# Induced attention with a maxout layer, one core: an output copy in four and two small additions go from ScalarE to VectorE

## The chip, the core and the metric

The kernel runs on one core of one Trainium2 chip. The metric is device time in microseconds (us) of one execution, as the median of repeated runs. The core's engines are TensorE (PE in the views, its weight loads PEld), VectorE (DVE), ScalarE (ACT), GpSimd (POOL) and SyncE (SP), which here issues transfers. They run side by side, each through its own list of instructions in order, and wait for each other by semaphores.

## The reference, cut to what matters

```python
def _attn_ref(x, inducing):                 # x: 4 x 12544 x 128, inducing: 32 x 128
    I = np.broadcast_to(inducing[None], (B, m, C))
    def mab(q, kv):
        s = scale * (q @ kv.transpose(0, 2, 1))
        s = s - s.max(-1, keepdims=True)
        a = np.exp(s)
        a /= a.sum(-1, keepdims=True) + 1e-09
        return a @ kv
    h = mab(I, x)
    return mab(x, h)

def _moe_ref(x, w1, w2, w3, w_out):         # x: 50176 x 128, w1..w3: 128 x 768, w_out: 768 x 128
    h = np.maximum(np.maximum(x @ w1, x @ w2), x @ w3)
    return h @ w_out
```

For each of four batches, 32 inducing vectors attend over 12544 tokens (the first attention); every token then attends over the 32 results (the second attention); and each token's result goes through a layer that keeps the largest of three products and multiplies it by `w_out`.

## The kernel before

**Slots.** The second attention's weights (32 numbers per token, as a high and a low part, in the tiles `pT`) are multiplied with matrices `us` made beforehand for the batch. The work is cut into chunks of 512 tokens and, within a chunk, into six slots (`j` from 0 to 5) of 128 hidden units. There are 600 slots. In each of them TensorE makes `pu` and `pv` (lines 790 and 800); ScalarE turns `pu` into `ru` with a Relu (809); VectorE takes the larger of `pv` and `ru` as `h` (830); ScalarE rounds `h` to `hi` (819); and the remainder `h - hi` goes into `lows`, which GpSimd makes for most slots (827) and VectorE for a few (833, by the tables `LOWVEC` and `LOWLAST`). Six slots later TensorE adds `hi` and `lows` times `w_out` up in `acc` (862 to 864). After a chunk's last slot, `finish` copies `acc` to `o` (875) and SyncE sends it out.

**Windows.** A batch is one short group of two 128-token tiles and six full groups of four chunks, of which the chunks count as `q` = 0 to 3. 24 slots make a window, in which one full group passes. I number the steps of a window 0 to 23. At fixed steps of it the attention work is put between the slots:

- the softmax of the second attention for the next group (`scores_steps`): transpose at step 3, maximum at 5, subtraction at 7, exponential on ScalarE at 8, row sums `rs` at 9, the addition of 1e-9 to `rs` at 10, reciprocal and multiplication at 11, transpose back at 13, rounding `ph` on ScalarE at 14, remainder `pl` at 15. In the last window of a batch two groups of the next batch pass through it, the short one a step earlier.
- the first attention of the next batch (not in the last batch): maximum, weights (449), transposes, sums, and `attend_add`, which adds a group's sums to the running ones: `hs` on VectorE (540), and the running sum of the weights in `lst` (543).
- TensorE's own part of the attention comes as bursts, the main one at step 2 (lines 696, 366, 502).

**Order.** All five lists are in the order in which the Python code calls the instructions. Within a step, `advance()` issues for ScalarE the next slot's `ru` and then the last slot's `hi`, and for VectorE `h` and then a `lows`, if there is one. After that comes `finish` of the chunk that has just ended (steps 0, 6, 12 and 18; `q` = 0 ends at step 12), and last the attention's entries for the step.

**Buffers that tie the engines.** `pu` and `pv` have two banks each: a slot's `pu` waits for the `ru` of two slots before, its `pv` for the `h` of two slots before. There are five buffers for `h`, ten for `hi`, eight for `lows`. `pu`, `pv`, `acc` and the attention's banks (`aux`) lie in PSUM; `ru`, `h`, `hi`, `lows`, `rs`, `lst` and `o` in SBUF.

Of the kernel before, what the change touches and what calls it, by code (L numbers as in the profile page):

```python
# [8 lines left out]
F32 = mybir.dt.float32  # L9
# [3 lines left out]
AF = mybir.ActivationFunctionType  # L13
ALU = mybir.AluOpType
# [11 lines left out]
def kernel(ctx, tc, x, xt, ind_t, w1, w2, w3, w_out, out):  # L26
    nc = tc.nc
# [3 lines left out]
    P = 128  # L31
# [19 lines left out]
    scale = 1.0 / float(C) ** 0.5  # L51
# [66 lines left out]
        (16, 10, "t", 3, 6),  # L118
    )
    LOWVEC = (23, 0, 15, 18)  # L120
    LOWLAST = (23, 0, 9, 15, 18)
    UW = 2 * DF + C
    UQ = UW // NQ

# [3 lines left out]
    while t0 < NT:  # L128
        nt = NT % GT if t0 == 0 and NT % GT else GT
# [6 lines left out]
    const = ctx.enter_context(tc.tile_pool(name="const", bufs=1))  # L136
# [55 lines left out]
    def first_load(what):  # L192
# [12 lines left out]
        out=sel[:, :M], in_=ident.rearrange("p (q m) -> p m q", m=M), axis=AX.X, op=ALU.add  # L205
    )
    nc.vector.tensor_copy(
        out=sel[:, M:].rearrange("p (q m) -> p q m", m=M),
        in_=sel[:, :M].unsqueeze(1).to_broadcast([P, NQ - 1, M]),
# [1 line left out]
    quad = const.tile([P, NQ], F32, name="quad")  # L211
    nc.vector.tensor_reduce(out=quad, in_=ident.rearrange("p (q m) -> p q m", m=M), axis=AX.X, op=ALU.add)

    eps = const.tile([P, 1], F32, name="eps")
    nc.gpsimd.memset(eps, 1e-9)

    bands = const.tile([P, NQ + 1, M], F32, name="bands")
    nc.gpsimd.memset(bands, 0.0)
# [152 lines left out]
    def opens(b, gi):  # L371

        return b > 0 and gi == 1
# [155 lines left out]
    def attend_add(b, gi):  # L529
        st = state[b]  # L530
        h = st["h"].pop(gi)
        if opens(b, gi):
            nc.scalar.copy(out=st["hs"], in_=h)
            if b == 1:
                st["l1"] = st["lst"][:, 1:2]
                return
            st["l1"] = st["lst"][:, :1]
            nc.scalar.activation(out=st["l1"], in_=st["l1"], func=AF.Identity, bias=st["lst"][:, 1:2])
            return
        nc.vector.scalar_tensor_tensor(  # L540
            out=st["hs"], in0=st["hs"], scalar=st["al"], in1=h, op0=ALU.mult, op1=ALU.add
        )
        nc.scalar.activation(
            out=st["l1"], in_=st["l1"], func=AF.Identity, scale=st["al"], bias=st["lst"][:, gi : gi + 1]
        )

    def add_quadrants(st):
# [133 lines left out]
    def sorted_(ap):  # L681

        return ap.rearrange("p (b a) -> p a b", a=2)

    def halves(ap):

        return ap.rearrange("p (a b) -> p a b", a=2)
# [13 lines left out]
    def scores_steps(b, gi):  # L701

        nt = groups[gi]["nt"]
        w = nt * M
        st = state[b]
        sp = st["s"].pop(gi)
        flat = sp[:, :w]
        ev = flat.rearrange("p (t m) -> p t m", m=M)
        nc.vector.transpose(out=flat, in_=flat)
        yield  # L710
        mx = wk.tile([P, GT], F32, name="mx", tag="mx")
        nc.vector.tensor_reduce(out=mx[:, :nt], in_=ev, axis=AX.X, op=ALU.max)
        yield
        nc.vector.tensor_sub(out=ev, in0=ev, in1=mx[:, :nt].unsqueeze(2).to_broadcast([P, nt, M]))
        yield
        nc.scalar.activation(out=flat, in_=flat, func=AF.Exp, scale=scale)
        yield
        rs = wk.tile([P, GT], F32, name="rs", tag="rs")
        nc.vector.tensor_reduce(out=rs[:, :nt], in_=ev, axis=AX.X, op=ALU.add)
        yield  # L720
        if b == 0 and gi < 2:
            nc.vector.tensor_scalar_add(out=rs[:, :nt], in0=rs[:, :nt], scalar1=1e-9)
        else:
            nc.scalar.activation(out=rs[:, :nt], in_=rs[:, :nt], func=AF.Identity, bias=eps)
        yield
        nc.vector.reciprocal(out=rs[:, :nt], in_=rs[:, :nt])
        nc.vector.tensor_mul(out=ev, in0=ev, in1=rs[:, :nt].unsqueeze(2).to_broadcast([P, nt, M]))
        yield
        if nt < GT:

            pn = wk.tile([P, nt, 2, 2, M], F32R, name="pn", tag="pn", bufs=1)
            e4 = ev.unsqueeze(2).to_broadcast([P, nt, 2, M])
            nc.scalar.copy(out=pn[:, :, :, 0, :], in_=e4)
            yield
            nc.vector.tensor_sub(out=pn[:, :, :, 1, :], in0=e4, in1=pn.bitcast(F32)[:, :, :, 0, :])
            st[("p", gi)] = pn
            yield
            return
        nc.vector.transpose(out=flat, in_=flat)
        yield  # L740
        ph = wk.tile([P, 512], F32R, name="ph", tag="ph")
        nc.scalar.copy(out=ph, in_=flat)
        yield
        pl = wk.tile([P, 512], F32R, name="pl", tag="pl")
        nc.vector.tensor_sub(out=pl, in0=flat, in1=ph.bitcast(F32))
        st[("p", gi)] = (ph.bitcast(F32), pl.bitcast(F32))
        yield
# [87 lines left out]
    class Chunk:  # L835
# [7 lines left out]
        def low(self, k):  # L843
# [3 lines left out]
            if self.b == 0 and self.gi == 1:  # L847
                return NJ * self.q + k in LOWVEC[:1]
            return NJ * self.q + k in (LOWVEC if self.b + 1 < B else LOWLAST)

# [14 lines left out]

    def finish(c):
        at = groups[c.gi]["at"] + (c.q or 0) * c.w
        turns = [(nc.vector.tensor_copy if c.n < 3 else nc.scalar.copy, nc.sync)]
        if len(c.acc) > 1:

            turns = [(nc.vector.tensor_copy, nc.sync), (nc.scalar.copy, nc.scalar)]
        for (acc, cs), (copy, queue) in zip(c.acc, turns):
            o = op.tile([P, 512], F32, name="o", tag="o", bufs=3)
            w = cs.stop - cs.start
            copy(out=halves(o[:, :w]), in_=sorted_(acc[:, :w]))  # L875
            queue.dma_start(out=out[c.b, :, at + cs.start : at + cs.stop], in_=o[:, :w])
# [27 lines left out]
    def softmax2(b, gi, *when):  # L904

        gen = []

        def step():
            if not gen:
                gen.append(scores_steps(b, gi))  # L910
            next(gen[0], None)

        for s in when:
            at(s, step)
# [60 lines left out]
    for n, turns in enumerate(TURNS, start=1):  # L975
        for gi, win, slot, wait, past in turns:
            s = begins(win) + slot
            if gi:
                burst(s, (attend_products, n, gi, bank_a[1]))
                if gi == 1:  # L980
                    burst(s, (attend_products, n, 0, None, 2 * P))
                    at(s + 1, keep_short, n)
                softmax1(n, gi, s, wait, calm=2 * narrow(s))
            for k, g in enumerate(past):
                burst(s, (attend_sums, n, g, None, k * P))
                at(s + 1 + (k if len(past) > 1 else narrow(s)), attend_add, n, g)
        s = begins(win) + (8 if slot < 8 else 20)
        at(s, add_quadrants, ("state", n))
        at(s, total_sums, ("state", n))
        at(s + 1, invert_total, ("state", n))  # L990
        at(s + 1, combine_states, ("state", n), 1)
# [160 lines left out]
```

## Time and profile before

| | |
|---|---|
| median of 3 runs | 790.11 us (790.03 to 791.17) |
| the profiled execution | 790.35 us |
| its span, first to last instruction | 788.5 us |
| TensorE busy | 774.7 us, 98% of the span |
| ScalarE busy | 727.1 us, 92% |
| VectorE busy | 639.4 us, 81% |
| GpSimd busy | 639.6 us, 81% |
| granted TensorE clock, mean | 0.999 |

The profile is of one execution. Busy time is the time in which an engine has at least one instruction under way. ScalarE's and VectorE's instructions overlap a little with the next one, so what an instruction takes up of its engine is the distance from its start to the next one's start where nothing is waited for. TensorE's matmuls are pipelined, so its busy share says little; there, too, the distance from start to start is what counts. Idle time in the views stands with what ended it.

### The profile page before, as it was taken

Reading aid. Unit: us, or ns where it says so; the run is one execution under the profiler, and the core shown is the slowest. Engines: PE = TensorE matmul, PEld = TensorE weight load, DVE = VectorE, ACT = ScalarE, POOL = GpSimd, SP = SyncE. Lnnn points to the kernel's source line nnn. Section 1 sums busy time; section 2 is a strip of 40 time slices with the busy share of each in tenths; the row PEclk is TensorE's granted clock in tenths of the full one; section 3 lists DMA queues with packets and bytes.
Section 4 is the critical chain, followed back from the end, with each engine's and each line's share of the span. In section 5 each row is a group of like instructions: output and inputs, shape, how many; then the busy total and the mean of one; then the engine's idle time right before and its main releaser. Section 6 shows DMA issues by size and latency. Waiting matters only on the chain.

```text
span 788.5 us, 14348 instructions
## 1 busy us (share of the span) xinstructions
PE 774.7 (98%) x4567; PEld 626.4 (79%) x4567; DVE 639.4 (81%) x1071; ACT 727.1 (92%) x1529; POOL 639.6 (81%) x523
## 2 busy tenths in 40 slices
PE   8999999999999999999999999999999999999998
PEld 6768878878787787787878877878888788787887
DVE  5898978878877787887887878878888788888876
ACT  5789899999998999998998999999999999999996
POOL 1379879878788897887987978879879989888887
PEclk9999999999999999999999999999999999999999
DMA  9744325274542643543644336334223222222221
GB/s 355 293 148 126 100 91 178 62 249 161 189 139 65 200 131 101 188 123 108 217 137 132 114 103 195 120 114 134 71 79 96 74 81 81 68 87 73 69 81 53
DMA packets 52266, 102.24 MB, mean 130 GB/s; under 512 B 18144, under 2 KB 21344, under 8 KB 46944
## 3 DMA queue, kind: packets, MB, share of 16 engines
q1 hardware_dynamic: 52048, 101.21, 40.5%
q8 instruction: 36, 0.59, 0.3%
q14 instruction: 38, 0.31, 0.1%
q10 hardware_dynamic: 144, 0.13, 0.0%
HBM read 48.12 MB, written 25.69 MB: 94 GB/s over the span
## 4 chain that ended last, share of the span: by engine, by line
PE 56%; ACT 33%; POOL 3%; DMA 3%; DVE 2%; issue 1%; SPq 0%; POOLq 0%; ACTq 0%; DVEq 0%
ACT ru L809 14%; ACT hi L819 13%; PE pu L790 10%; PE acc L862 9%; PE pv L800 9%; PE acc L863 9%; PE acc L864 9%; PE aux L696 3%; POOL lows L827 3%; ACT o L875 2%; PE acc L502 2%; DMA raw<-in_w_dram 2%; PE aux L366 2%; PE acc L861 2%; ACT aux L449 1%
## 5 line engine op out<-in xcount | busy, mean ns | idle before, releaser
L827 POOL TENSOR_TENSOR lows<-h,hi 128x512 fp32r<-128x512 f32 (+1 forms) x504 | 624.4, 1275 | 112.4 <-ACT hi L819 109.3
L830 DVE TENSOR_TENSOR h<-pv,ru 128x512 f32<-128x512 f32 (+1 forms) x600 | 400.9, 673 | 123.8 <-PE pv L800 63.0
L809 ACT ACTIVATE ru<-pu 128x512 f32<-128x512 f32 (+1 forms) x600 | 407.0, 679 | 37.8 <-PE pu L790 37.5
L819 ACT CAST hi<-h 128x512 fp32r<-128x512 f32 (+1 forms) x596 | 416.3, 699 | 0.3 <-DVE h L830 0.2
L790 PE MATMUL pu<-pT,us 128*128 128x512 f32 (+1 forms) x600 | 229.2, 382 | 4.5 <-ACT ru L809 3.7
L800 PE MATMUL pv<-pT,us 128*128 128x512 f32 (+1 forms) x600 | 226.6, 378 | 1.6 <-DVE h L830 1.5
L862 PE MATMUL acc<-hi,wo_hi 128*128 128x512 f32 (+1 forms) x594 | 225.5, 380 | 0.0
L863 PE MATMUL acc<-hi,wo_lo 128*128 128x512 f32 (+1 forms) x594 | 222.6, 375 | 0.0
L864 PE MATMUL acc<-lows,wo_hi 128*128 128x512 f32 (+1 forms) x594 | 222.6, 375 | 0.0
L790 PEld LDWEIGHTS pu<-pT,us 128*128 128x128 f32 x600 | 113.2, 189 | 37.8 <-ACT ru L809 18.8
L862 PEld LDWEIGHTS acc<-hi,wo_hi 128*128 128x128 f32 x594 | 112.2, 189 | 21.9 <-issue 7.5
L800 PEld LDWEIGHTS pv<-pT,us 128*128 128x128 f32 x600 | 113.4, 189 | 19.6 <-DVE h L830 6.6
L864 PEld LDWEIGHTS acc<-lows,wo_hi 128*128 128x128 f32 x594 | 112.3, 189 | 15.3
L863 PEld LDWEIGHTS acc<-hi,wo_lo 128*128 128x128 f32 x594 | 112.3, 189 | 14.7
L833 DVE TENSOR_TENSOR lows<-h,hi 128x512 fp32r<-128x512 f32 x96 | 87.7, 913 | 0.8 <-ACT hi L819 0.8
L875 ACT COPY o<-acc 128x512 f32<-128x512 f32 (+1 forms) x96 | 65.3, 680 | 0.0
L861 PE MATMUL acc<-pT,us 128*128 128x512 f32 (+1 forms) x99 | 37.3, 376 | 0.0
L502 PEld LDWEIGHTS acc<-xg,aT 128*32 128x32 f32 x640 | 18.0, 110 | 9.6 <-issue 5.4
L696 PE MATMUL aux<-xT,hT 128*32 128x512 f32 x192 | 25.1, 603 | 0.0
L366 PE MATMUL aux<-xT,iT 128*32 128x512 f32 x184 | 24.1, 596 | 0.2 <-ACT pT L768 0.2
L502 PE MATMUL acc<-xg,aT 128*32 128x128 f32 x640 | 21.4, 273 | 0.1
L861 PEld LDWEIGHTS acc<-pT,us 128*128 128x128 f32 x99 | 18.7, 189 | 2.6 <-DVE hs L540 0.2
(163 smaller groups left out, 445.6 us busy)
## 6 DMA issues: line engine op xcount, KB each, us to landing
out_dram<-o SPq DMA_DIRECT2D x95, 256.0 KB, 2.2
xg<-in_x_dram SPq DMA_DIRECT2D x23, 1024.0 KB, 6.1
xT<-in_xt_dram SPq DMA_DIRECT2D x18, 1024.0 KB, 5.5
pT<-ph SPq DMA_DIRECT2D x190, 64.0 KB, 2.0
pT<-pl SPq DMA_DIRECT2D x190, 64.0 KB, 2.0
raw<-in_w_dram SPq DMA_DIRECT2D x3, 768.0 KB, 8.7
us<-uh SPq DMA_DIRECT2D x24, 52.0 KB, 1.9
us<-ul SPq DMA_DIRECT2D x24, 52.0 KB, 2.5
```

Of the source, the lines that this page charges most:

```text
L790: nc.tensor.matmul(out=pu[:, :w], lhsT=state[c.b]["us"][:, 2 * j * P : (2 * j + 1) * P], rhs=turned(c.pT[:, :w]), start=True, stop=True,)
L800: nc.tensor.matmul(out=pv[:, : d.w], lhsT=state[d.b]["us"][:, (2 * j + 1) * P : (2 * j + 2) * P], rhs=turned(d.pT[:, : d.w]), start=True, ...
L809: nc.scalar.activation(out=halves(ru[:, :w]), in_=sorted_(pu[:, :w]), func=AF.Relu)
L819: nc.scalar.copy(out=hi[:, : c.w], in_=h[:, : c.w])
L827: nc.gpsimd.tensor_sub(**args)
L830: nc.vector.tensor_max(out=halves(h[:, : d.w]), in0=sorted_(pv[:, : d.w]), in1=halves(relus.pop(s)[:, : d.w]))
L833: nc.vector.tensor_sub(**low)
L861: nc.tensor.matmul(out=to, lhsT=us[:, 2 * DF :], rhs=turned(c.pT[:, cs]), start=True, stop=False)
L862: nc.tensor.matmul(out=to, lhsT=wo_hi[:, row_of(j), :], rhs=turned(c.hh[j][:, cs]), start=False, stop=False)
L863: nc.tensor.matmul(out=to, lhsT=wo_lo[:, row_of(j), :], rhs=turned(c.hh[j][:, cs]), start=False, stop=False)
L864: nc.tensor.matmul(out=to, lhsT=wo_hi[:, row_of(j), :], rhs=turned(c.hl[j][:, cs]), start=False, stop=(j == NJ - 1))
L875: copy(out=halves(o[:, :w]), in_=sorted_(acc[:, :w]))
```

## The change

Four things change. The addition of 1e-9 to the row sums `rs` is made by VectorE for every group, where ScalarE made it for all but the first two. The running sum of the first attention's weights is updated by VectorE instead of ScalarE. VectorE copies the output of chunks with `q` = 0; before, it did so only for the first three chunks and half of the last. And in the last batch, `LOWLAST` gives VectorE the low part at slot 7 of a window in the place of that at slot 9. The tile `eps` and its memset on GpSimd fall away. Work per engine: VectorE has 66 instructions more (26 additions to `rs`, 17 updates of the sum, 23 copies), ScalarE 66 fewer.

```diff
-    LOWLAST = (23, 0, 9, 15, 18)
+    LOWLAST = (23, 0, 7, 15, 18)
...
-    eps = const.tile([P, 1], F32, name="eps")
-    nc.gpsimd.memset(eps, 1e-9)
...
             st["l1"] = st["lst"][:, :1]
-            nc.scalar.activation(out=st["l1"], in_=st["l1"], func=AF.Identity, bias=st["lst"][:, 1:2])
+            nc.vector.tensor_add(out=st["l1"], in0=st["l1"], in1=st["lst"][:, 1:2])
             return
...
-        nc.scalar.activation(
-            out=st["l1"], in_=st["l1"], func=AF.Identity, scale=st["al"], bias=st["lst"][:, gi : gi + 1]
+        nc.vector.scalar_tensor_tensor(
+            out=st["l1"], in0=st["l1"], scalar=st["al"], in1=st["lst"][:, gi : gi + 1], op0=ALU.mult, op1=ALU.add
         )
...
-        if b == 0 and gi < 2:
-            nc.vector.tensor_scalar_add(out=rs[:, :nt], in0=rs[:, :nt], scalar1=1e-9)
-        else:
-            nc.scalar.activation(out=rs[:, :nt], in_=rs[:, :nt], func=AF.Identity, bias=eps)
+        nc.vector.tensor_scalar_add(out=rs[:, :nt], in0=rs[:, :nt], scalar1=1e-9)
...
-        turns = [(nc.vector.tensor_copy if c.n < 3 else nc.scalar.copy, nc.sync)]
+        turns = [(nc.vector.tensor_copy if c.n < 3 or c.q == 0 else nc.scalar.copy, nc.sync)]
```

How the lists read, first on VectorE in a window in the middle of batch 1, steps 9 to 13 (`aux` is the bank of the softmax, `rs` its row sums). Before:

```order
L719 TENSOR_REDUCE rs_4141<-aux0_79 128x16
L830 TENSOR_TENSOR h_4153<-pv0_83,ru_4134 128x512
L830 TENSOR_TENSOR h_4173<-pv1_84,ru_4148 128x512
L726 RECIPROCAL rs_4141<-rs_4141 128x16
L727 TENSOR_TENSOR aux0_79<-aux0_79,rs_4141 128x512
L830 TENSOR_TENSOR h_4187<-pv0_83,ru_4168 128x512
L830 TENSOR_TENSOR h_4203<-pv1_84,ru_4182 128x512
L739 STREAM_TRANSPOSE aux0_79<-aux0_79 128x512
```

The same place on VectorE in the changed kernel:

```order
L717 TENSOR_REDUCE rs_4139<-aux0_79 128x16
L825 TENSOR_TENSOR h_4151<-pv0_83,ru_4132 128x512
L719 TENSOR_SCALAR rs_4139<-rs_4139 128x16
L825 TENSOR_TENSOR h_4171<-pv1_84,ru_4146 128x512
L721 RECIPROCAL rs_4139<-rs_4139 128x16
L722 TENSOR_TENSOR aux0_79<-aux0_79,rs_4139 128x512
L825 TENSOR_TENSOR h_4185<-pv0_83,ru_4166 128x512
L870 COPY o_4187<-acc0_85 128x512
L825 TENSOR_TENSOR h_4201<-pv1_84,ru_4180 128x512
L734 STREAM_TRANSPOSE aux0_79<-aux0_79 128x512
```

Two rows have come in: the addition to `rs` between the `h` of step 10 and that of step 11, and the copy of `o` between the `h` of step 12 and that of step 13. On ScalarE the same two stood, before, at steps 10 and 12:

```order
L724 ACTIVATE rs_3759<-rs_3759,eps_100 128x16
L809 ACTIVATE ru_3786<-pu0_81 128x512
L819 CAST hi_3788<-h_3771 128x512
L809 ACTIVATE ru_3800<-pu1_82 128x512
L819 CAST hi_3802<-h_3791 128x512
L875 COPY o_3807<-acc0_85 128x512
```

In the changed kernel the first and the last of these rows are gone, and `ru` and `hi` alternate without a break. In the last batch VectorE's list also has the moved low part. Before, steps 9 to 12 of its window 1 (windows of a batch count from 0):

```order
L719 TENSOR_REDUCE rs_8836<-aux0_79 128x16
L830 TENSOR_TENSOR h_8847<-pv0_83,ru_8829 128x512
L830 TENSOR_TENSOR h_8865<-pv1_84,ru_8843 128x512
L833 TENSOR_TENSOR lows_111<-h_8834,hi_8845 128x512
L726 RECIPROCAL rs_8836<-rs_8836 128x16
L727 TENSOR_TENSOR aux0_79<-aux0_79,rs_8836 128x512
L830 TENSOR_TENSOR h_8880<-pv0_83,ru_8860 128x512
```

The same place after the change, from the `lows` of step 9 on:

```order
L828 TENSOR_TENSOR lows_109<-h_8806,hi_8816 128x512
L717 TENSOR_REDUCE rs_8834<-aux0_79 128x16
L825 TENSOR_TENSOR h_8846<-pv0_83,ru_8826 128x512
L719 TENSOR_SCALAR rs_8834<-rs_8834 128x16
L825 TENSOR_TENSOR h_8864<-pv1_84,ru_8841 128x512
L721 RECIPROCAL rs_8834<-rs_8834 128x16
L722 TENSOR_TENSOR aux0_79<-aux0_79,rs_8834 128x512
L825 TENSOR_TENSOR h_8878<-pv0_83,ru_8859 128x512
L870 COPY o_8880<-acc0_85 128x512
```

The `lows` has gone from in front of the reciprocal to in front of the row sums, two steps earlier.

## Rows read from the trace of the kernel before

**Rows 1.** Waits over the span: who waited for whom, us, times, longest.

```profile
PEld pu L790 <- ACT ru L809: 18.8, 49, 0.7
```

**Rows 2.** Chain that ended last, 300 to 335 us: start, us, what.

```profile
302.50 1.00 PE aux L696 x8
...
327.12 0.50 ACT ru L809
...
332.93 1.00 PE aux L696 x8
```

**Rows 3.** Timeline of PE in that window: start, us, instruction, [idle before].

```profile
314.97 0.38 PE L800 MATMUL pv<-pT,us 128*128 128x512 f32 x1
315.19 0.38 PE L862 MATMUL acc<-hi,wo_hi 128*128 128x512 f32 x1
...
326.98 0.38 PE L864 MATMUL acc<-lows,wo_hi 128*128 128x512 f32 x1
327.66 0.48 PE L790 MATMUL pu<-pT,us 128*128 128x512 f32 x1 [0.31 <-ACT ru L809]
```

**Rows 4.** Timeline of ACT, steps 10 to 14 of the same window.

```profile
315.56 0.38 ACT L724 ACTIVATE rs<-rs,eps 128x16 f32<-128x16 f32 x1
...
317.75 0.68 ACT L875 COPY o<-acc 128x512 f32<-128x512 f32 x1
318.23 0.70 ACT L809 ACTIVATE ru<-pu 128x512 f32<-128x512 f32 x1
...
320.22 0.70 ACT L742 CAST ph<-aux 128x512 fp32r<-128x512 f32 x1
```

**Rows 5.** Timeline of DVE, steps 10 to 13 of the same window.

```profile
314.53 0.68 DVE L830 TENSOR_TENSOR h<-pv,ru 128x512 f32<-128x512 f32 x1
315.49 0.69 DVE L830 TENSOR_TENSOR h<-pv,ru 128x512 f32<-128x512 f32 x1 [0.27 <-PE pv L800]
316.09 0.24 DVE L726 RECIPROCAL rs<-rs 128x16 f32<-128x16 f32 x1
316.37 0.70 DVE L727 TENSOR_TENSOR aux<-aux,rs 128x512 f32<-128x512 f32 x1
316.98 0.68 DVE L830 TENSOR_TENSOR h<-pv,ru 128x512 f32<-128x512 f32 x1
...
318.47 0.72 DVE L739 STREAM_TRANSPOSE aux<-aux 128x512 f32<-128x512 f32 x1
```

**Rows 6.** Timeline of POOL in that window; one row holds 13 instructions.

```profile
307.50 16.21 POOL L827 TENSOR_TENSOR lows<-h,hi 128x512 fp32r<-128x512 f32 x13 [1.76 <-ACT hi L819]
```

**Rows 7.** Timeline of DVE at 49.7 us.

```profile
49.71 0.86 DVE L817 CAST hi<-h 128x256 fp32r<-128x256 f32 x1
```

**Rows 8.** Timeline of POOL at 49.7 us.

```profile
49.69 0.73 POOL L827 TENSOR_TENSOR lows<-h,hi 128x256 fp32r<-128x256 f32 x1 [0.36 <-ACT hi L819]
```

**Rows 9.** All CASTs of line 817: ns minimum/median/maximum, first and last start, forms.

```profile
L817 DVE CAST hi<-h x4: 294/360/860, 48.2 to 53.6; 128x256 fp32r<-128x256 f32 x3, 128x512 fp32r<-128x512 f32 x1
```

**Rows 10.** Groups by line and shape: count | busy us, mean ns | idle before.

```profile
L252 DVE TENSOR_SCALAR pw<-t 128x768 uint32<-128x768 uint32 x4 | 2.2, 545 | 0.0
...
L875 DVE COPY o<-acc 128x512 f32<-128x512 f32 x2 | 1.4, 678 | 0.0
```

**Rows 11.** Timelines of DVE in windows 1 and 2 of the last batch, step 11.

```profile
655.23 1.32 DVE L833 TENSOR_TENSOR lows<-h,hi 128x512 fp32r<-128x512 f32 x1
...
684.68 0.68 DVE L833 TENSOR_TENSOR lows<-h,hi 128x512 fp32r<-128x512 f32 x1
```

**Rows 12.** Timeline of DVE in the last window of batch 0, step 10.

```profile
216.80 0.68 DVE L830 TENSOR_TENSOR h<-pv,ru 128x512 f32<-128x512 f32 x1
```

**Rows 13.** Timeline of POOL in the last window of batch 0.

```profile
214.85 7.48 POOL L827 TENSOR_TENSOR lows<-h,hi 128x512 fp32r<-128x512 f32 x6
```

**Rows 14.** Timeline of DVE in the first window of batch 1, step 10.

```profile
253.48 0.68 DVE L830 TENSOR_TENSOR h<-pv,ru 128x512 f32<-128x512 f32 x1
```

**Rows 15.** Timeline of POOL in the first window of batch 1.

```profile
246.85 16.19 POOL L827 TENSOR_TENSOR lows<-h,hi 128x512 fp32r<-128x512 f32 x13 [1.35 <-ACT hi L819]
```

## The prediction, made before the changed kernel was run

> **What bounds the kernel now.** I read the waits over the span first, then the chain that ended last in a window in the middle of batch 1, then the timelines of the engines there. In the waits the reader should see that TensorE's load for `pu` waits for ScalarE's `ru`, 18.8 us in 49 pieces [rows 1]. A load normally stands one matmul ahead of its own, and matmuls start 0.22 apart (314.97 and 315.19) [rows 3], so of each piece 0.22 costs TensorE nothing: 18.8 - 49 x 0.22 = 8 us are lost, and up to 0.1 more behind each piece, where the next load is late in turn. That is 8 to 13 us, and I take 10 as the most that a relieved ScalarE can give back.
>
> From one main burst to the next such a window takes 30.43 us [rows 2]. The loss in it falls late: at 327.66 `pu` starts 0.68 after the matmul before it instead of 0.22 [rows 3], behind the `ru` on which the chain stood until then [rows 2]. With the small pieces beside it I count 0.7 in the window. So ScalarE is the bound, and only from step 16 or so on; the steps before count as far as they make ScalarE later there. There are nine such plain windows: 1 to 3 of batches 0, 1 and 2.
>
> **What ScalarE is relieved of.** The copy of `o` holds it 0.48 (317.75 to 318.23), the addition to `rs` is 0.38 long and overlaps its neighbours, so I take 0.2 [rows 4]; the `lst` update I price the same. That is 0.9 a window, more than the 0.7 that is lost. If VectorE did its new work free of charge, the 0.7 would go.
>
> **What VectorE pays.** The memset of `eps` that goes stands in the set-up and gets nothing, either way. The copy of `o` is 0.68 long on VectorE [rows 10] and takes 0.60 of it, as `h`, equally long, does (316.37 to 316.98 for a neighbour of 0.70) [rows 5].
>
> The addition to `rs` is the open price: no row of the trace shows it beside a GpSimd operation that lasts. From below it costs 0.1. From above it waits until GpSimd's running operation ends. That such waits exist, rows 7 to 9 show: a CAST of VectorE from SBUF to SBUF starts 0.02 after a `lows` of GpSimd, which ends at 50.42, and takes until 50.57, 0.86 instead of 0.29 [rows 7 to 9]. VectorE's own `lows`, with two inputs in SBUF, takes 0.68 or 1.32 in the same place of two windows [rows 11]. `h` and the copy of `o`, which read PSUM, hold to 0.68 or 0.69. Which of them is the addition like? It reads one tensor in SBUF and writes SBUF, like the CAST, and TENSOR_SCALAR also has the CAST's pace: 0.545 for 768 elements against 0.294 for 256 is 0.49 ns an element [rows 9, 10], where `h` with 512 in 0.68 cannot go below 1 ns. It is nearest to the CAST, so I take the wait, and keep 0.1 as the other end. The `lst` update has two SBUF inputs like `lows`; I take the wait for it too.
>
> The Trainium skill bears on this choice: "SBUF — State Buffer", section "Who interferes with whom", lists copy, cast and tensor_scalar as able to enter VectorE's 2-port modes, in which they and GpSimd shut each other out for a whole instruction, and adds instructions with two SBUF inputs. The CAST's 0.86 and the `lows` of 1.32 agree; for the addition no run here shows it. By that rule the sum is the one below with the wait.
>
> **How long it waits in a plain window.** GpSimd's 13 operations from 307.50 fill 16.21 without a gap, 1.247 each, so the seventh lasts from 314.98 to 316.23 or a little more [rows 6]. The addition stands behind the `h` of step 10, which began at 314.53 and passes VectorE on at 315.13 [rows 5]: 0.15 into that operation. With the wait, `h` of step 11 starts at about 316.3 instead of 315.49. From there VectorE has no gap: 0.60 to the reciprocal, 0.28, 0.61 (both as now [rows 5]), 0.60 for `h`, 0.60 for `o`, 0.60 for `h`, so the transpose starts at 319.6 instead of 318.47, and ends, 0.72 long, at 320.3. ScalarE's `ph` rounds that transpose's output. It stands at 320.22 now [rows 4], would come near 319.5 by the relief alone, and starts at 320.3 with the wait. Behind `ph`, ScalarE's list is as before. All that was gained is gone at this point: **+0.1 a window, and 9 x 0.1 = +0.9**. TensorE loses some 0.4 here, since `pv` of steps 15 and 16 waits for the late `h`, but that is taken out of the wait for ScalarE that follows, not added to it. The wait for `lst` comes at step 3, when what is late is made good by step 9.
>
> Without the wait, 0.27 of idle time before the `h` of step 11 hides the addition [rows 5]; the copy of `o` moves the transpose from 318.47 to 316.98 + 3 x 0.60 = 318.8, `ph` comes at 319.6, and 0.6 of the 0.7 is won.
>
> **The other windows, with the wait.**
> - First windows of batches 1 and 2: the short group shifts GpSimd. Its sixth operation from 246.85 on ends at about 246.85 + 6 x 1.245 = 254.3 [rows 15], and the addition would come at 253.48 + 0.60 = 254.08 [rows 14]. It waits 0.25, which the idle time there hides, and the relief holds: -0.6 each, **-1.2**.
> - Last windows of batches 0, 1 and 2 have two additions. The first stands ahead of the `h` at 216.80, in GpSimd's second operation from 214.85, which lasts until about 217.37 [rows 12, 13]: 0.55 of wait. The second, 0.60 behind that `h`, falls to the start of the third: 0.7 more. Then come two reciprocals and `o`. From the start of a `pv` to its `h` pass 0.52 (314.97 and 315.49 [rows 3, 5]), `h` takes 0.68, and two slots (ten matmuls of 0.216) pass until the bank is wanted again: 2.16 - 0.52 - 0.68 leaves 0.9 in which a late `h` costs nothing. Here `h` is up to 1.6 late and more behind `o`, and I put TensorE's loss at 1.1, in the place of 0.4 lost to ScalarE there now: +0.7 each, **+2.1**.
> - Last batch: `lows` at step 11 takes 1.32 in window 1, with the reciprocal's work behind it, and 0.68 in window 2 [rows 11]; by start to start, windows 0, 1 and 3 lose 0.7, 0.6 and 1.0 us there, 2 and 4 nothing. Moved to step 9 it still waits for GpSimd, half an operation in windows 0, 1 and 3 (I give back 0.3 each, the rest goes to the copy of `o` behind), but nearly a whole one in 2 and 4 (0.8 each, new): **+0.6**, between -1.5 and +2.
> - The rest: the first window of batch 0, where VectorE has no gap, +0.5; the fifth windows of three batches +0.25 together: **+0.75**.
>
> The sum is 0.9 - 1.2 + 2.1 + 0.6 + 0.75 = +3.15. Against the profiled execution's 790.35 (span 788.5 and 1.85 around it) that is 793.5; the median of the runs is 0.24 lower, so **793.2 us**.
>
> **Rivals.**
> - *The additions don't wait* (the other side). Then the plain windows give 9 x 0.6 = 5.4, the first windows of batches 1 and 2 0.9 each, the last windows 0.45 each and the fifth 1.1: 9.7 in all, 780.4. It turns on one thing, whether an addition of 16 elements in SBUF holds off until GpSimd is through; the point from which it decides is a wait of about 0.4 in the plain windows, under which `ph` comes earlier than now. For it: the short RECIPROCAL beside it takes 0.24 in every window. Against it: the CAST. Chance 0.2. The Trainium skill's "ScalarE: Activation LUTs", section "Rules for kernel authors", puts adds and multiplies on VectorE and so points this way; no run here shows it.
> - *They wait, but shorter than priced*, because the phases shift as TensorE moves; then part of the relief stays. Half the wait in the plain windows and no new loss at the batch ends: 793.2 - 9 x 0.4 - 2.1 = 787.5. This covers 787 to 791.7. Chance 0.25.
> - *VectorE becomes the bound in the last batch as well*, its lateness running on from window to window: the upper ends above, +2 more there and another 2 in the fifth and last windows, 797 or over. Chance 0.07.
> - The change doing something other than it says I put at nothing: the lists show each instruction in its new place.
>
> **How the numbers follow.** The forecast holds with 0.48, from 791.7 to 797. The likeliest time is its 793.2, and its own range 790.5 to 797. The range of all cases, 779.5 to 797, takes in the first rival's 780.4 and leaves out its lower part and the third rival. A measurement of this kernel tells 0.2%, 1.6 us, from no change. Faster than 788.5: 0.2 for the first rival and 0.1 of the second, 0.30. Within 1.6 us: 0.15 of the second and 0.05 of the forecast's lower edge, 0.20. Slower: 0.50.
>
> **What would show it.** The rows of the addition to `rs` in the plain windows: 1.1 to 1.2 us long if the step holds, under 0.2 if not. `ph` there no earlier against the burst than now, about 17.7 us behind it. ScalarE's busy time down by some 25 us, and the wait of the `pu` load for `ru` smaller by half, with as much in `pv` loads that wait for `h`. In the last batch, `lows` of step 9 at about 1.3 in windows 2 and 4. The prediction is wrong if the additions are short, or if the late transposes don't reach `ph`.

## The result, and the profile after

The changed kernel takes 795.37 us (median of 4 runs, 795.23 to 796.89) against 790.35 for the kernel before on the same chip: ratio 1.0066, 95% interval 1.0049 to 1.0084, so 5.0 us slower. The profiled execution took 795.34, with a span of 793.6. Two of the six runs of one experiment, the copies alone, fell in a slower state (811.0 and 813.7 us) and are left out of its time and ratio.

The page of the changed kernel, where lines 719, 785, 795 and 825 are the addition to `rs`, `pu`, `pv` and `h`:

```profile
PE 782.6 (99%) x4567; PEld 622.9 (78%) x4567; DVE 670.9 (85%) x1137; ACT 718.4 (91%) x1463; POOL 641.5 (81%) x522
...
L795 PEld LDWEIGHTS pv<-pT,us 128*128 128x128 f32 x600 | 113.1, 188 | 44.0 <-DVE h L825 30.8
L785 PEld LDWEIGHTS pu<-pT,us 128*128 128x128 f32 x600 | 113.3, 189 | 24.7 <-ACT ru L804 7.3
...
L719 DVE TENSOR_SCALAR rs<-rs 128x16 f32<-128x16 f32 (+1 forms) x28 | 21.1, 755 | 0.1
```

ScalarE did get lighter (727.1 before, 718.4 now), and the load of `pu` waits for `ru` 7.3 us where it waited 18.8 [rows 1]. What came in its place is the load of `pv`, which waits 30.8 us for `h`, where the kernel before had this row:

```profile
PEld pv L800 <- DVE h L830: 6.6, 18, 1.1
```

VectorE is late. An addition of 16 elements per partition (of 2 in four cases) costs 0.755 us on average. The minimum, median and maximum of the two small operations that went to VectorE, in ns (the `lst` update is line 541):

```profile
L719 DVE TENSOR_SCALAR rs<-rs x28: 155/730/1239, 42.5 to 745.4; 128x16 f32<-128x16 f32 x24, 128x2 f32<-128x2 f32 x4
```

```profile
L541 DVE SCALAR_TENSOR_TENSOR lst<-lst,al x15: 210/697/1341, 88.1 to 562.0; 128x1 f32<-128x1 f32 x15
```

Now the window that [rows 2 to 6] showed, window 2 of batch 1. Its burst and the next, by the chain of the changed kernel:

```profile
305.45 0.99 PE aux L694 x8
...
336.11 0.98 PE aux L694 x5
```

It lasts 30.66 instead of 30.43. VectorE in it (310.20 and 322.77 are the two transposes, 311.06 the `lst` update, 318.42 the addition, 321.58 the copy of `o`):

```profile
310.20 0.72 DVE L707 STREAM_TRANSPOSE aux<-aux 128x512 f32<-128x512 f32 x1
310.83 0.30 DVE L538 SCALAR_TENSOR_TENSOR hs<-hs,al,acc 128x128 f32<-128x128 f32 x1
311.06 0.70 DVE L541 SCALAR_TENSOR_TENSOR lst<-lst,al 128x1 f32<-128x1 f32 x1
311.68 0.68 DVE L825 TENSOR_TENSOR h<-pv,ru 128x512 f32<-128x512 f32 x1
...
315.26 0.68 DVE L712 TENSOR_TENSOR aux<-aux,mx 128x512 f32<-128x512 f32 x1
...
317.82 0.68 DVE L825 TENSOR_TENSOR h<-pv,ru 128x512 f32<-128x512 f32 x1
318.42 1.17 DVE L719 TENSOR_SCALAR rs<-rs 128x16 f32<-128x16 f32 x1
319.50 0.68 DVE L825 TENSOR_TENSOR h<-pv,ru 128x512 f32<-128x512 f32 x1
...
321.58 0.68 DVE L870 COPY o<-acc 128x512 f32<-128x512 f32 x1
322.18 0.68 DVE L825 TENSOR_TENSOR h<-pv,ru 128x512 f32<-128x512 f32 x1
322.77 0.72 DVE L734 STREAM_TRANSPOSE aux<-aux 128x512 f32<-128x512 f32 x1
```

and ScalarE's `ph` and TensorE's load for `pv` beside them, which waits for `h`:

```profile
323.53 0.59 ACT L737 CAST ph<-aux 128x512 fp32r<-128x512 f32 x1
```

```profile
321.72 0.19 PEld L795 LDWEIGHTS pv<-pT,us 128*128 128x128 f32 x1 [0.36 <-DVE h L825]
```

Count from each window's burst. `h` of step 10 starts 12.37 behind it (12.03 before, [rows 2, 5]), `h` of step 11 14.05 (12.99), the transpose 17.32 (15.97), `ph` 18.08 (17.72, [rows 4]). `ph` starts as the transpose ends (322.77 + 0.72). So `ph` is 0.36 later, the window 0.23 longer. Part of the lateness, 0.34, is there before the addition begins.

Window by window, from the first `pu` of a window to that of the next, the 5.0 us are: plain windows +1.7 (eight at +0.23, window 1 of batch 0 at -0.15), first windows of batches 1 and 2 +1.0, last windows of batches 0 to 2 +1.5, fifth windows +2.2, first window of batch 0 +0.65, last batch -1.6, the short windows between batches -0.4.

### The profile page after: what moved, and what is told of

The parts are those of the page before. It is cut to its first block, busy times and chain, and to the rows that moved or that the text cites. A ratio compares the mean times of both kernels' runs of the same rounds, so it can differ in the third digit from the quotient of the medians.

```text
span 793.6 us, 14393 instructions
## 1 busy us (share of the span) xinstructions
PE 782.6 (99%) x4567; PEld 622.9 (78%) x4567; DVE 670.9 (85%) x1137; ACT 718.4 (91%) x1463; POOL 641.5 (81%) x522
## 4 chain that ended last, share of the span: by engine, by line
PE 85%; ACT 8%; DVE 3%; DMA 2%; issue 1%; POOL 1%; POOLq 0%; SPq 0%; DVEq 0%; ACTq 0%
PE pv L795 16%; PE acc L857 14%; PE pu L785 14%; PE acc L858 14%; PE acc L859 14%; ACT hi L814 3%; ACT ru L804 3%; PE aux L694 3%; PE acc L500 2%; PE acc L856 2%; PE aux L364 2%; DVE h L825 2%; DMA xg<-in_x_dram 1%; POOL lows L822 1%; DMA raw<-in_w_dram 1%
## 5 line engine op out<-in xcount | busy, mean ns | idle before, releaser
L804 ACT ACTIVATE ru<-pu 128x512 f32<-128x512 f32 (+1 forms) x600 | 375.2, 626 | 39.8 <-PE pu L785 39.6
L814 ACT CAST hi<-h 128x512 fp32r<-128x512 f32 (+1 forms) x596 | 384.3, 645 | 11.1 <-DVE h L825 9.4
L795 PE MATMUL pv<-pT,us 128*128 128x512 f32 (+1 forms) x600 | 234.3, 391 | 2.6 <-DVE h L825 1.7
L795 PEld LDWEIGHTS pv<-pT,us 128*128 128x128 f32 x600 | 113.1, 188 | 44.0 <-DVE h L825 30.8
L828 DVE TENSOR_TENSOR lows<-h,hi 128x512 fp32r<-128x512 f32 x96 | 85.6, 892 | 0.8 <-ACT hi L814 0.8
L870 ACT COPY o<-acc 128x512 f32<-128x512 f32 (+1 forms) x73 | 45.2, 620 | 0.0
L719 DVE TENSOR_SCALAR rs<-rs 128x16 f32<-128x16 f32 (+1 forms) x28 | 21.1, 755 | 0.1
```

The lines of the kernel that those rows point to most:

```text
L795: nc.tensor.matmul(out=pv[:, : d.w], lhsT=state[d.b]["us"][:, (2 * j + 1) * P : (2 * j + 2) * P], rhs=turned(d.pT[:, : d.w]), start=True, ...
L804: nc.scalar.activation(out=halves(ru[:, :w]), in_=sorted_(pu[:, :w]), func=AF.Relu)
L814: nc.scalar.copy(out=hi[:, : c.w], in_=h[:, : c.w])
L828: nc.vector.tensor_sub(**low)
```

## The experiments

Every time is set against runs of the kernel before on the same chip (789.9 to 790.3 us). "Plain window" is window 2 or 3 of a batch, 30.43 before and 30.66 in the changed kernel. First, each suspected cost undone or done by itself.

**The additions alone** (from the kernel before):

```diff
-        if b == 0 and gi < 2:
-            nc.vector.tensor_scalar_add(out=rs[:, :nt], in0=rs[:, :nt], scalar1=1e-9)
-        else:
-            nc.scalar.activation(out=rs[:, :nt], in_=rs[:, :nt], func=AF.Identity, bias=eps)
+        nc.vector.tensor_scalar_add(out=rs[:, :nt], in0=rs[:, :nt], scalar1=1e-9)
```

> The kernel before with one part of the change alone: every addition to the row sums stands on VectorE. Theory of the wait: the addition takes 1.1 to 1.2 us in the plain windows, `h` of step 11 starts 0.8 later, and nothing else is eased but ScalarE's 0.2 to 0.4 a window, so the time goes up against the kernel before, to 792 to 797 us. Rival, the load: VectorE's added busy time (mostly the copies of `o`) is what ate the relief; then an addition of 0.1 alone gives 788 to 790.5.

791.57 us, ratio 1.0017 (1.0008 to 1.0026): slower, just under the range of the theory and above that of the rival. The additions take as long as in the changed kernel (median 0.93, at most 1.24), yet a plain window is 30.24, shorter than before: without the copy of `o` behind it VectorE makes up for half of the 0.8, `ph` comes 0.2 earlier than before, and ScalarE's relief is won. The loss lies in the last batch (+1.6 over the kernel before), in the first window of batch 0 (+0.7), and in the fifth and last windows (+0.5 and +0.4 over three batches).

**The additions back on ScalarE, and no additions at all** (from the changed kernel):

```diff
-        nc.vector.tensor_scalar_add(out=rs[:, :nt], in0=rs[:, :nt], scalar1=1e-9)
```

In the first of the two kernels the four lines of the kernel before, with the branch for the first two groups, come in its place; in the second nothing does.

> The changed kernel with the additions to the row sums back on ScalarE (the first two of batch 0 stay on VectorE, as before); copies of `o`, the running sum of the weights and slot 7 stay as changed. Theory of the wait: the 1.16 us of the addition are gone, ScalarE is still rid of the copy (0.48) and of the `lst` update, and the time falls under that of the kernel before, 783 to 788 us. Rival, the load on VectorE: its busy time falls by some 21 us only where nothing waits for it, and the time stays at 793 to 796.

> The changed kernel without the addition of 1e-9 to the row sums on any engine (left out of the computation: the sum has the largest weight, exp of 0, in it, so 1e-9 is below its last place). Theory of the wait: neither wait nor work, so the relief of ScalarE is won: 780 to 784 us, near the 780.4 of the rival without waits. Rival, the load on VectorE: 792 to 795.

On ScalarE again: 788.38, ratio 0.9977 (0.9968 to 0.9986). Without any: 785.57, ratio 0.9943 (0.9929 to 0.9956). Both are faster than the kernel before, so the additions turn a gain into the loss; but both are slower than the theory's range, so they are not all that eats the relief.

**The same addition in another form** (from the changed kernel; `rs2` holds 1e-9 in its second column):

```diff
-        nc.vector.tensor_reduce(out=rs[:, :nt], in_=ev, axis=AX.X, op=ALU.add)
+        rs2 = rs2s[(b * len(groups) + gi) % 4][:, :nt, :]
+        nc.vector.tensor_reduce(out=rs2[:, :, 0], in_=ev, axis=AX.X, op=ALU.add)
...
-        nc.vector.tensor_scalar_add(out=rs[:, :nt], in0=rs[:, :nt], scalar1=1e-9)
+        nc.vector.tensor_reduce(out=rs[:, :nt], in_=rs2, axis=AX.X, op=ALU.add)
```

> The changed kernel with the same addition on VectorE in another form: the row sum is written beside a constant column of 1e-9, and a reduction over the two columns (TENSOR_REDUCE, 16 by 2 elements in SBUF) takes the place of the TENSOR_SCALAR. Theory of the wait by the kind of instruction: the reduction takes under 0.25 us beside a running `lows` of GpSimd, as RECIPROCAL does, and the time is that without the addition plus at most 2 us: 780 to 786 us. Rivals: any small operation from SBUF to SBUF waits there, then it takes 1.1 to 1.2 us as well and the time is that of the changed kernel, 794 to 797; or the load on VectorE decides, then 793 to 796 with a short reduction.

786.25 us, ratio 0.9953 (0.994 to 0.9965), just above the theory's range. All its additions in ns, minimum, median, maximum:

```profile
L725 DVE TENSOR_REDUCE rs<-rs x28: 146/174/186, 42.4 to 737.2; 128x16 f32<-128x32 f32 x24, 128x2 f32<-128x4 f32 x4
```

None waits. The same arithmetic at the same place of the same queue costs 0.17 instead of 0.73 and the kernel is 9 us faster. So it is not VectorE's load, and not any small operation from SBUF to SBUF: the TENSOR_SCALAR form waits, the TENSOR_REDUCE form does not. The Trainium skill, "SBUF — State Buffer", section "Who interferes with whom", has a tensor_reduce on this chip never contend with GpSimd and a tensor_scalar able to; the trace agrees, with 0.15 to 0.19 for the one and up to 1.24 for the other.

**The running sum of the weights**, back on ScalarE in the changed kernel, and alone on VectorE in the kernel before:

```diff
+        nc.scalar.activation(
+            out=st["l1"], in_=st["l1"], func=AF.Identity, scale=st["al"], bias=st["lst"][:, gi : gi + 1]
+        )
-        nc.vector.scalar_tensor_tensor(
-            out=st["l1"], in0=st["l1"], scalar=st["al"], in1=st["lst"][:, gi : gi + 1], op0=ALU.mult, op1=ALU.add
-        )
```

> The changed kernel with the running sum of the weights back on ScalarE; the additions to the row sums stay on VectorE. Theory of the wait: the 0.70 us (1.34 in the first windows of batches 1 and 2) that the update waits beside `lows` are gone from VectorE; the first windows get their 0.4 to 0.6 back, the plain windows 0.1 to 0.2 each at the price of ScalarE's busy time, and the addition's wait stays: 790 to 793.5 us. Rival, made good by step 9 as predicted: only the first windows of batches 1 and 2 change and ScalarE gets its load back: 794 to 796.

> The kernel before with the running sum of the weights alone on VectorE. By the prediction's working the wait comes at step 3 of a plain window and is made good by step 9, and ScalarE is rid of 0.2 to 0.38: 788 to 790.5 us. Rival, the wait costs wherever it falls, 0.7 in the plain windows and 1.3 in the first ones of batches 1 and 2: 791 to 795.

Alone on VectorE: 796.73 us, ratio 1.0085 (1.0072 to 1.0098), more than the whole change costs, for 17 updates of one element per partition. The rival held, and its range was still too low. Window 2 of batch 1, first the bursts, then VectorE (the update stands in line 543), then ScalarE with `ph`:

```profile
305.26 0.99 PE aux L696 x8
...
336.20 0.99 PE aux L696 x8
```

```profile
310.87 0.69 DVE L543 SCALAR_TENSOR_TENSOR lst<-lst,al 128x1 f32<-128x1 f32 x1
...
315.07 0.68 DVE L714 TENSOR_TENSOR aux<-aux,mx 128x512 f32<-128x512 f32 x1
...
318.60 0.69 DVE L830 TENSOR_TENSOR h<-pv,ru 128x512 f32<-128x512 f32 x1 [0.28 <-ACT ru L809]
```

```profile
309.09 0.60 ACT L809 ACTIVATE ru<-pu 128x512 f32<-128x512 f32 x1 [1.94 <-PE pu L790]
...
312.25 0.62 ACT L819 CAST hi<-h 128x512 fp32r<-128x512 f32 x1 [0.41 <-DVE h L830]
...
323.54 0.67 ACT L742 CAST ph<-aux 128x512 fp32r<-128x512 f32 x1
```

The subtraction of the maximum and ScalarE's first `ru` behind the burst in the kernel before:

```profile
311.78 0.69 DVE L714 TENSOR_TENSOR aux<-aux,mx 128x512 f32<-128x512 f32 x1
```

```profile
306.32 0.60 ACT L809 ACTIVATE ru<-pu 128x512 f32<-128x512 f32 x1 [1.93 <-PE pu L790]
```

The window is 30.94, 0.51 longer. The subtraction of the maximum starts 9.81 behind the burst, in the changed kernel as here, against 9.28 before, and `ph` 18.28 behind it, against 17.72. VectorE makes more than half of its lateness good: it has idle time again before the `h` of step 11 (318.60), and its second transpose starts 16.19 behind the burst, 0.22 later than before. ScalarE does not. Its `hi` waits 0.41 for the `h` behind the update (312.25), and from its first `ru` to `ph` it needs 14.45 instead of 13.90, though it has one operation fewer. `ph` does not wait for the transpose here, which has ended 1.37 earlier; it comes late because ScalarE is late. A wait of 0.41 or 0.42 stands at this place in windows 2 and 3 of all batches of the five profiled kernels with the update on VectorE, and in none of the other nine.

With the update back on ScalarE, the changed kernel's ten runs lie between 790.0 and 796.1, median 793.02, ratio 1.0037 (1.002 to 1.0055), in the theory's range. A plain window falls to 30.33, and `ph` comes 0.34 earlier, so the cost of the update is confirmed there. But the profiled run, at 795.75, has one window of 33.88 that none of its edits explains. VectorE's low part in it, TensorE behind it, and the granted clock (the column after POOL) in four stretches:

```profile
451.60 4.47 DVE L828 TENSOR_TENSOR lows<-h,hi 128x512 fp32r<-128x512 f32 x1
```

```profile
456.72 0.80 PE L795 MATMUL pv<-pT,us 128*128 128x512 f32 x1 [2.66 <-DVE h L825]
457.31 0.63 PE L857 MATMUL acc<-hi,wo_hi 128*128 128x512 f32 x1
457.73 0.63 PE L858 MATMUL acc<-hi,wo_lo 128*128 128x512 f32 x1
```

```profile
452.00:454.00 2.00, 2.00 (x10) 1.47 (x8) 2.00 (x1) 2.00 (x5) 2.00 (x2) 1.00 1.01 310
...
456.00:460.00 4.00, 3.28 (x8) 2.65 (x9) 2.83 (x7) 3.03 (x7) 0.94 (x1) 0.51 0.66 229
460.00:462.80 2.80, 2.80 (x8) 2.23 (x7) 1.79 (x3) 1.66 (x4) 1.83 (x3) 0.50 0.08 24
463.00:470.00 7.00, 7.00 (x69) 4.82 (x68) 3.87 (x6) 4.68 (x9) 3.70 (x3) 1.00 0.25 75
```

A subtraction of 0.68 took 4.47. Behind the idle time that it made, TensorE ran at 0.50 to 0.51, its 1.2 GHz level, its matmuls 0.43 apart instead of 0.216, until 462.85.

**Neither of the two waits, and the copies alone.** The first is the changed kernel without the addition and with the update on ScalarE; the second is the kernel before with this line:

```diff
-        turns = [(nc.vector.tensor_copy if c.n < 3 else nc.scalar.copy, nc.sync)]
+        turns = [(nc.vector.tensor_copy if c.n < 3 or c.q == 0 else nc.scalar.copy, nc.sync)]
```

> The changed kernel with neither of the two waits: no addition to the row sums at all (the 1e-9 is left out), the running sum of the weights on ScalarE; only the copies of `o` and slot 7 stay of the change. Theory that the wait of the update costs as well: 781 to 784.5 us, under the 785.6 of the kernel that only lacks the addition, most of it in the first windows of batches 1 and 2. Rival, the update's place doesn't matter (its wait is made good, its busy time on ScalarE costs as much): 785 to 787.

> The kernel before with the copies of `o` alone moved (one in four to VectorE). `o` reads PSUM and took 0.68 beside a running `lows`, so it waits for nothing: ScalarE is rid of 0.48 a window at the price of 0.60 of VectorE where it has 0.27 of slack. Theory that this is the part that gains: 0.3 of the 0.7 that is lost in a plain window, 785 to 788 us. Rival, the transpose that it moves by 0.3 eats the relief: 789 to 791.

Both theories and both rivals failed. Without the two waits: 798.44 us, ratio 1.0101 (1.0086 to 1.0116). The copies alone: a median of 798.4, its runs scattered from 793.1 to 802.9, ratio 1.0103 (1.0066 to 1.014). And yet their best windows are the shortest so far, 29.7 and 29.9 for plain ones. The others are 32.1 to 33.8 (34.6 for a fifth window), each behind a `lows` of VectorE that took 3.95 to 4.5 us, seven of them in the first kernel and four in the second. One in the first kernel, on VectorE, with GpSimd's queue beside it and TensorE behind:

```profile
324.07 0.69 DVE L824 TENSOR_TENSOR h<-pv,ru 128x512 f32<-128x512 f32 x1 [0.28 <-PE pv L794]
324.68 3.95 DVE L827 TENSOR_TENSOR lows<-h,hi 128x512 fp32r<-128x512 f32 x1
328.56 0.68 DVE L824 TENSOR_TENSOR h<-pv,ru 128x512 f32<-128x512 f32 x1
```

```profile
309.40 18.68 POOL L821 TENSOR_TENSOR lows<-h,hi 128x512 fp32r<-128x512 f32 x15 [1.76 <-ACT hi L813]
331.63 2.52 POOL L821 TENSOR_TENSOR lows<-h,hi 128x512 fp32r<-128x512 f32 x2 [3.55 <-ACT hi L813]
```

```profile
326.79 0.38 PE L784 MATMUL pu<-pT,us 128*128 128x512 f32 x1
329.29 0.48 PE L794 MATMUL pv<-pT,us 128*128 128x512 f32 x1 [2.11 <-DVE h L824]
329.61 0.38 PE L856 MATMUL acc<-hi,wo_hi 128*128 128x512 f32 x1
329.82 0.38 PE L857 MATMUL acc<-hi,wo_lo 128*128 128x512 f32 x1
```

The reader should set the first two fences beside each other. GpSimd works without a gap from 309.40 to 328.08, fifteen operations. VectorE's `lows`, at slot 15, starts at 324.68, in the thirteenth, which is that of slot 14, and ends 0.55 after the fifteenth: two further operations of GpSimd, those of slots 16 and 17, went ahead of it. Their inputs were not there yet when VectorE's `lows` started: the two `hi` end at 325.13 and 326.14, each before GpSimd has ended what it has under way. Then GpSimd has nothing to do for 3.55, because VectorE did not make its inputs. In the profile this wait has no releaser; it shows only as a length. The matmuls here go on 0.22 apart. That is so in both windows of 32.1 of this kernel; in the four of 33.8, with the same stop of TensorE of 2.11 to 2.13, a stretch at a granted clock of 0.50 follows, in that of 33.3 behind a stop of 2.65.

All fourteen traces together have 26 `lows` of VectorE of over 2.3 us, and in each case GpSimd's next input was there before the operation under way ended. Where it was not there, in 634 cases, none took that long; but of those where it was there 183 did not either.

**The slots of VectorE's low parts.** GpSimd takes 1.245 us for an operation [rows 15] and a slot lasts 1.08, so it falls 0.165 behind in each slot that it has alone. That would be 2.3 us over slots 1 to 14, nearly two operations, and the expectations below go by it; in the window above it is less, as the operation of slot 14 starts 1.21 behind the end of its `hi`, one operation. First slot 7 alone in the last batch, in the kernel before; then, in the kernel without the two waits, an earlier slot taken from GpSimd in every batch:

```diff
-    LOWVEC = (23, 0, 15, 18)
+    LOWVEC = (23, 0, 7, 15, 18)
```

> The kernel before with VectorE's low part of the last batch at slot 7 instead of 9, and nothing else. Theory from the windows of the last batch (138.5 us for the first five in the changed kernel, 139.8 in the kernel before): slot 7 falls where GpSimd's queue has run less behind, `lows` waits less, and the last batch gains 1 to 2 us: 788 to 789.3 us. Rival, the prediction's term: windows 2 and 4 lose what 0, 1 and 3 win, 789.8 to 791.5.

> The kernel without the addition and with the update on ScalarE (798.4 us, its windows 29.7 us long or, behind a `lows` of VectorE that took 3.95 us at slot 15, 32.1 to 33.8) with VectorE's low parts of batches 0 to 2 at slots 23, 0, 7, 15 and 18, as in the last batch (the 1e-9 is left out as there). Theory that the 3.95 is two more operations of GpSimd that were queued, and went first: with slot 7 taken from it GpSimd is an operation less behind at slot 15, no `lows` takes over 2 us there, and all windows come near 29.7: 775 to 783 us. Rival, GpSimd going first whenever the two meet: a new long wait at slot 7, 795 or over. Second rival, VectorE's 0.68 to 1.3 more a window: 784 to 790.

> As the kernel with slots 23, 0, 7, 15 and 18, with 23, 0, 6, 12 and 18 instead (the 1e-9 left out). Theory of the queue: GpSimd takes 1.25 us an operation where a slot lasts 1.08, so it is 0.17 further behind with each slot that it has alone; five slots in a row (0.85) are less than one slot behind, so VectorE's `lows` waits for one operation at most: no `lows` over 1.4 us, windows of 29.5 to 29.9 us, 775 to 782 us. Rival, the wait falls in VectorE's tight steps 10 to 16 and delays the transpose: 784 to 792.

Slot 7 alone: 789.27, ratio 0.9989 (0.998 to 0.9998). The interval just leaves out no change; its last batch is 0.8 shorter, and the time 0.7.

With slots 7, 15 and 18: 782.39, ratio 0.9906 (0.9892 to 0.992), 16 us under the same kernel without slot 7. Its low parts at slots 7, 15 and 18 in window 2 of batch 1 and GpSimd beside them:

```profile
310.47 0.68 DVE L827 TENSOR_TENSOR lows<-h,hi 128x512 fp32r<-128x512 f32 x1
...
319.32 1.30 DVE L827 TENSOR_TENSOR lows<-h,hi 128x512 fp32r<-128x512 f32 x1
...
322.75 0.80 DVE L827 TENSOR_TENSOR lows<-h,hi 128x512 fp32r<-128x512 f32 x1
```

```profile
304.04 6.29 POOL L821 TENSOR_TENSOR lows<-h,hi 128x512 fp32r<-128x512 f32 x5 [1.77 <-ACT hi L813]
311.33 11.68 POOL L821 TENSOR_TENSOR lows<-h,hi 128x512 fp32r<-128x512 f32 x9 [1.00 <-ACT hi L813]
```

GpSimd comes to rest for 1.00 in the middle of the window, so it is less far behind at slot 15 (its operation of slot 14 starts 0.90 behind its `hi`), and the low part there takes 1.30. Apart from one of 3.63 at 80.3, which the kernel before has as well, none takes over 1.5; plain windows are 29.85. That agrees with the theory in that GpSimd is less late and no long wait is left. It does not show why VectorE goes first here: the input of slot 16 is there 0.17 before GpSimd ends the operation under way. The time ends within the theory's range and not at its lower end, as the fifth and last windows did not gain.

Slots 6, 12 and 18 gave 791.03, ratio 1.0011 (1.0002 to 1.002): the rival's range, but not by its way, as the second transpose is not late. The low part at slot 12 takes 1.69 in the plain windows, behind that transpose; the `h` after it comes a microsecond late, ScalarE's `hi` waits 0.56 for it, and the windows become 30.58. The forecast of 1.4 at most was wrong there, and the place in VectorE's chain counts as well.

**The whole computation, best of each.** Reduction form, update on ScalarE, copies one in four, slots 7, 15 and 18:

> The whole computation with the best of each part: the addition of 1e-9 as a reduction over two columns on VectorE, the update of the running sum on ScalarE, the copies of `o` one in four on VectorE, and VectorE's low parts at slots 23, 0, 7, 15 and 18 in every batch. Theory: the reduction waits for nothing and costs 0.7 us in all as before, so 782 to 784 us, faster than both kernels. Rival: the phase between VectorE and GpSimd moves by 0.1 in each window and a `lows` loses the port twice again, 788 or over.

783.86 us, ratio 0.9919 (0.9906 to 0.9933): 6.4 us faster than the kernel before and 11.5 faster than the changed one, as the theory had it.

## Why the prediction was right, and where it was not

The forecast of 793.2, slower, with its own range to 797, holds the 795.37. Its mechanism was right for the addition and for ScalarE, but its terms erred in both directions: four came out 5.1 us too low together and three 3.2 too high. That the forecast came within 2.2 us of the time is in good part luck.

- **ScalarE is the bound and is relieved**: right. The wait of `pu` for `ru` fell from 18.8 to 7.3; in the plain windows without a long wait for GpSimd, with the update on ScalarE and the copies on VectorE, the relief shows as 0.5 to 0.7 (29.7 to 29.9), as large as the 0.7 that was counted. ScalarE's busy time fell only 8.7 and not 25; where the rest went was not taken apart.
- **The addition waits for GpSimd's operation**: right, 1.17 us in plain windows against 1.1 to 1.2 foretold, and shown by the reduction form to be the wait of this form of instruction. `ph` follows the late transpose as foretold. Over thirteen kernels the plain window without a long wait goes with `ph`: counted from the burst's first matmul (0.07 ahead of the chain's row) `ph` is 17.2 to 17.4 behind it in windows of 29.7 to 29.9, 17.6 to 17.9 in those of 30.2 to 30.5, 18.15 in that of 30.66 and 18.35 in that of 30.94. The kernel with slots 6, 12 and 18 falls out of this (17.20 and 30.58): its wait comes behind `ph`.
- **"The wait for `lst` comes at step 3, when what is late is made good by step 9"**: wrong. This is the step that failed. It followed VectorE alone, which does make more than half of it good; but ScalarE, which the prediction itself has as the bound, waits 0.41 for the `h` behind the update and has next to no idle time up to `ph` in which to make that good. Alone, the update costs 0.51 a plain window and 6.7 us in all; in the changed kernel putting it back gives 0.33 a plain window. It is what turned the plain windows from about -0.1 (30.33 without it) to +0.23, and 1.7 in all where 0.9 stood.
- **First windows of batches 1 and 2**: -1.2 foretold, +1.0 measured. The addition took 0.71, so waited some 0.5 and not 0.25, because the update took 1.34 there. With the update on ScalarE and the addition alone on VectorE it took 0.30 in these windows, and they gained 0.4 together. The update starts at 250.32, just before the first of the three GpSimd operations in the row below ends; it did not get in then, but behind the second:

```profile
250.32 1.34 DVE L541 SCALAR_TENSOR_TENSOR lst<-lst,al 128x1 f32<-128x1 f32 x1
```

```profile
249.12 3.76 POOL L822 TENSOR_TENSOR lows<-h,hi 128x512 fp32r<-128x512 f32 x3 [1.42 <-ACT hi L814]
```

- **Last windows**: +2.1 foretold, +1.5 measured; **first window of batch 0**: +0.5, +0.65. Right in sign. The two additions of a last window are 0.59 and 0.73 long, where waits of 0.55 and 0.7 were priced.
- **Fifth windows**: +0.25 foretold, +2.2 measured. The term was mis-sized. In that of batch 2 the addition starts 0.07 into an operation of GpSimd and takes 1.24, almost the longest wait there can be behind one operation. Without the addition these windows are as before (93.51 us together, 93.50 before).
- **Last batch**: +0.6 foretold, -1.6 measured, at the other end of its own bounds (-1.5). `lows` at slot 7 took 1.03 in window 1 (1.32 before, [rows 11]) and 0.68 in windows 2 and 4, where 1.3 was feared. The five additions there took 0.15 to 0.32. Half of the 1.6 is slot 7 alone (0.8).
- **The additions don't wait**, the rival on the other side, fell by the rows. Its time of 780.4 was not reached by leaving the addition out either: that kernel stayed at 785.6, as the update still waited, and 782.4, the best of all, needed the update on ScalarE and slot 7 as well.

What the prediction did not see at all is that a relief can make things worse. In the changed kernel the waits make `h` and `hi` late as well, so that GpSimd's operation of slot 16 starts as its input arrives (0.08 behind it) and `lows` at slot 15 gets in ahead of it, 1.12 long in the window shown. When both waits are taken out, that `lows` waits for three operations and all is lost, with TensorE's clock at times on top. Such a wait at slot 15 was seen in three kernels, all with the copies on VectorE, the update on ScalarE and `LOWVEC` as before.

Open: which of two waiting engines goes first when GpSimd ends an operation and its next input is there. In the kernel with the copies alone that input was there 0.27 to 0.29 before the end in nine windows; four of their `lows` at slot 15 lost twice, five got in at once (1.47 to 1.49), and starts 0.34 to 0.37 into the operation are found on both sides. No rule follows from these. That the scatter of the copies-alone runs is this wait was seen in the one profiled run only.

## What to carry to other kernels

Before a small operation goes to VectorE beside a GpSimd that works without gaps, ask which form it has: here an addition of 16 elements took 0.17 as a reduction and up to 1.24 as a TENSOR_SCALAR, and an update of one element per partition with two SBUF inputs took 0.69 to 1.34 beside one. Price such a wait at the engine that bounds the kernel: look which of its instructions needs what stands behind the wait in VectorE's queue, and call the wait made good only where that engine, and not VectorE alone, has idle time afterwards. Where VectorE shares a stream of work with GpSimd, give it its parts early and often enough that GpSimd runs out of inputs between them; a part taken when GpSimd's next input is already there can wait for several operations, here up to four.

## What the runs showed that was not expected

- A wait of VectorE for GpSimd is not bounded by one operation: 3.95 us behind three in a row, and 4.47 behind four in another kernel, for an operation of 0.68. The kernel before has one such row, too, 3.63 long at 80.6.
- After a stop of TensorE of 2.66 us the granted clock of the next 6 us was 0.50 to 0.51, the 1.2 GHz level. After stops of 2.11 to 2.13 it fell to 0.50 in four windows of the kernel without the two waits, and not at all in two others.
